# Squares and product stores moved to ScalarE's side, and two pieces of work one step sooner

## The chip, the core and the metric

The kernel runs on one core of one Trainium2 chip. Its time is the device time of that core in microseconds (us), the median of three runs. The engines are TensorE (PE; its weight loads are shown apart as PEld), VectorE (V, or DVE), ScalarE (A, or ACT), GpSimd (G, or POOL) and SyncE (SP). Before the change SP issues every DMA of the program.

## What is computed

The reference has three parts, all in float32:

```python
def sm_attn(qq, kk, vv):
    s = scale * np.matmul(qq, kk.transpose(0, 1, 3, 2))
    s = s - np.max(s, axis=-1, keepdims=True)
    a = np.exp(s)
    a = a / (np.sum(a, axis=-1, keepdims=True) + 1e-09)
    return np.matmul(a, vv)
p_packed = sm_attn(p, k, v)
out = sm_attn(q, p_packed, p_packed)
...
h = np.maximum(x @ w_in, 0.0)
x = h * h @ w_out
...
h = x @ w_in
...
solu = h * sm
...
return (ln @ w_out).astype(np.float32)
```

The attention has 8 batches, 8 heads, 576 positions of 64 numbers, and 32 packed positions. Its output, 4608 tokens of 512 numbers, goes through a first MLP (hidden width 2048, Relu squared) and a second one (hidden width 1024, softmax times h, a layer norm with gains). The weights come as float64 and are decoded to float32 on the chip.

## The kernel before, in words

A float32 matmul is made of three faster ones: each operand is split in a high part (fp32r, a rounded copy) and a low part (the rest), and the products high x high, low x high and high x low are summed. So each operand costs a rounded copy (mostly ACT) and a subtraction (DVE or POOL, `split_lo`, line 55).

**The first MLP's input weights are multiplied by the packed positions' values.** The attention's second half is a matrix `a` (softmax of the queries against 32 packed positions per head) times a small matrix. The kernel multiplies this small matrix by w_in beforehand. A `Unit` (lines 262 to 306) does this for a half `g` of the heads, a slice `s` of 512 columns of w_in and a group `bg` of four batches: it loads a piece of w_in (`raw`), decodes it in three steps (`Decode`, lines 105 to 133: one ACT instruction L122, three DVE instructions L123, L127, L129, then `fin` with a copy on ACT L271 and a subtraction on POOL), and when its `done` time and the packed values allow, `product()` runs 12 matmuls (`pw`), two evacuations on ACT (L293) and two subtractions on DVE (L294). Its result `pws` is stored one step later, from the list `later`: four DMAs of 256 KB to DRAM (`pw_d`), or for slices 0 and 1 of batch 0 four of 64 KB straight into the `slot` tile and three to DRAM (`store`, lines 297 to 306). `load_slot` reads a slice of a batch back from DRAM. There are 16 units for each group of batches; those of group 0 begin at the steps listed in line 514, those of group 1 every second step from step 92 on (line 629).

**The steps.** The main loop (lines 811 to 867) counts t; a step of the first MLP is i = t - 10. At each t the order in which the program is written is: the stores of `later`; the packed attention of batches 0 to 3 (`K0`: `scores`, `soft`, `transp`, `packed`, `pairs`, for t up to 9); `products()`; then `h1` of step i (six matmuls `h`, Relu on ACT L413, r x r on POOL L414, Square into the high part on ACT L415, subtraction on DVE L55); the jobs listed for that t (loads, decodes, softmax jobs); `products()` again; and `ymm` of step i - 4 (12 matmuls `Y`, lines 419 to 443; `LAG` is 4). There are 256 steps: batches 0 and 1 alternate at first, two or four hidden blocks at a time, so step 8 is the first of batch 1.

**The softmax jobs** of a batch `b` and a half `g` (`s2_jobs`, lines 329 to 395) are single instructions or a few: load, scores (`s`), max, subtraction, exponential, sum, normalisation, back-transposition, and the copies to `ah` and `al`, which `h1` reads. For batch 0 they run on DVE, for the others the subtraction, normalisation and low part run on POOL. The jobs of batch 0, half 1 are cut in two parts; the first nine of them are written at t = 9, the others at i = 0. Those of batch 1 are written three at each step from i = 2 to 7 (lines 863 to 865).

**Order.** Instructions wrapped in `pin` (`tc.keep_in_program_order`, line 43) stay behind the instruction that is written just before them for the same engine; these are nearly all matmuls, all DMAs (`dma`, line 51), and ACT's L122 and L293. A planner orders the others by its own model of time. The unit's ready time is in two lines:

```python
self.done = clock[0] + (1 if clock[0] < T0 else 2)   # fin, line 273
return self.done and clock[0] >= self.done and (self.bg, 2 * self.g + 1) in L
```

and `unit_at` (lines 469 to 479) puts a unit's decode steps k, k and k + 1 steps behind its beginning. The units of slice 1 begin at i = -5 (the entries -5 of line 514, written at t = 5).

Of the kernel before, what the change touches and what calls it, by code (L numbers as in the profile page):

```python
# [15 lines left out]
AF = mybir.ActivationFunctionType  # L16
ALU = mybir.AluOpType
# [14 lines left out]
def f(ap):  # L32
    return ap.bitcast(F32)


def build(tc, qT, kT, vP, pT, w_in, w_out, w_in2, w_out2, g_ln, out):
    nc = tc.nc

    TURN = {n: cycle(x) for n, x in {"ETC": "VVA", "LNA": "AAAV"}.items()}
    V, A, G, PE, SP = nc.vector, nc.scalar, nc.gpsimd, nc.tensor, nc.sync  # L40


    pin = tc.keep_in_program_order

    def mm(*a, **k):
        pin(PE.matmul(*a, **k))  # L46

    def flip(own, *a):
        (pin if own else lambda x: x)(PE.transpose(*a))

    def dma(out, in_):
        pin(SP.dma_start(out=out, in_=in_))

    def split_lo(eng, lo, x, hi):
        eng.tensor_tensor(out=lo, in0=x, in1=f(hi), op=ALU.subtract)  # L55

    def pool(name, side="left", space=None):
        st = ExitStack()
        kw = dict(space=space) if space is not None else dict(side=side)
        return st.enter_context(tc.tile_pool(name=name, bufs=1, **kw)), st  # L60
# [3 lines left out]
    pw_d = dr.tile([B, 8, P, 2, 512], F32, name="pw_d")  # L64
# [6 lines left out]
    def bank(name):  # L71
        return ps.tile([P, 512], F32, tag="a", name=name, bufs=4)
# [26 lines left out]
    def t25(k, name, dt=F32):  # L99
        return mp.tile([P, KC * P], dt, tag="e" + k, name=name, bufs=2 if k == "1" else 4)  # L100
# [4 lines left out]
    class Decode:  # L105
        def __init__(self, pl, src, shape, fin, bufs=(3, 2, 3)):
            self.pl, self.shape, self.fin, self.n, self.bufs = pl, shape, fin, 0, bufs
            self.raw = pl.tile([P, shape[0], shape[1], 2], U32, tag="raw", name="raw", bufs=bufs[0])
            dst = self.raw.rearrange("p a c w -> p a (c w)")
            dma(dst if shape[0] > 1 else dst[:, 0, :], src)  # L110
# [33 lines left out]
    class Pack:  # L144
# [71 lines left out]
        def transp(self, n):  # L216
            t = self.pl.tile([P, KC * P], F32, tag="eT", name="eT", bufs=2) if self.own else t25("2", "eT")
            self.eT[n] = t.rearrange("p (k c) -> p k c", k=KC)
            for a, b in ((0, 3), (3, KC)):
                pt = bank("pt")[:, :(b - a) * P]  # L220
                for c in range(a, b):
                    flip(self.own, pt[:, (c - a) * P:(c - a + 1) * P], self.e1[n % 2][:, c * P:(c + 1) * P], ident)
                if next(TURN["ETC"]) == "A":
                    A.copy(t[:, a * P:b * P], pt)
# [37 lines left out]
    class Unit:  # L262
# [34 lines left out]
        def store(self, sf):  # L297
            bg, s, g = self.bg, self.s, self.g
            for b4 in range(4):
                r = slice(32 * b4, 32 * b4 + 32)  # L300
                if bg == b4 == 0 and s < 2:
                    o = f(slot[0, s].rearrange("p g c l x -> p g (c l x)"))
                    for h in range(4):
                        dma(o[32 * h:32 * h + 32, g], sf[r, h])
                else:
                    dma(pw_d[4 * bg + b4, s, :, g].rearrange("(h p) c -> p h c", h=4), sf[r])

    def new_slot(b, s):
        slot[b, s] = big4(ring[0], [P, 2, 2, 2, P], "slot", F32R)
# [90 lines left out]
    def h1(n):  # L400
        b, half, fc = n
        c = slice(half * HF, (half + 1) * HF)
        pb = bank("h1")
        w = slot[b, fc // 2][:, :, fc % 2]
        i = 0
        for g in range(2):
            ah, al = at[b, g]
            for l, x in ((0, ah), (1, ah), (0, al)):
                mm(pb[:, :HF], w[:, g, l], x[:, c], start=(i == 0), stop=(i == 5))
                i += 1  # L410
        rg, g2 = t25("1", "rg"), t25("2", "ghl", F32R)
        r, gg, gh, gl = rg[:, :HF], rg[:, HF:S], g2[:, :HF], g2[:, HF:S]
        A.activation(r, pb[:, :HF], AF.Relu)  # L413
        G.tensor_tensor(out=gg, in0=r, in1=r, op=ALU.mult)  # L414
        A.activation(gh, r, AF.Square)  # L415
        split_lo(V, gl, gg, gh)
        gt[n] = (gh, gl)

    def ymm(n):
        b, half, fc = n  # L420
        gh, gl = gt.pop(n)
        wh, wl = wo[fc]
        firsts = cuts.get(b, whole)
        for oc in range(4):
            o = slice(oc * P, (oc + 1) * P)
            for i, (w, x) in enumerate(((wh, gh), (wl, gh), (wh, gl))):
                mm(Y[oc], w[:, o], x, start=(fc in firsts and i == 0), stop=(fc + 1 in firsts and i == 2))
        if fc + 1 in firsts:
            c0 = b * S + half * HF
            new = (b, half) not in yp  # L430
            if new:
                yp[b, half] = ypp.tile([P, 4 * HF], F32, name=f"yp{half}") if b == 1 else sums()
            t = yp[b, half]
            for oc in range(4):
                o = t[:, oc * HF:(oc + 1) * HF]
                if not new:
                    V.tensor_tensor(out=o, in0=Y[oc], in1=o, op=ALU.add)  # L437
                elif oc % 2 == 0:
                    A.copy(o, Y[oc])
                else:  # L440
                    V.tensor_copy(o, Y[oc])
            if fc == 15:
                later.append(lambda: dma(y_d[:, :, c0:c0 + HF], t.rearrange("p (o c) -> p o c", o=4)))
# [14 lines left out]
    def at_step(i, fn):  # L458
        jobs.setdefault(i if i == "first" else T0 + i, []).append(fn)
# [9 lines left out]
    def unit_at(i, bg, s, g, pl, bufs):  # L469
        d = {}  # L470

        def begin():
            d["u"] = Unit(bg, s, g, pl(), bufs)
            queue.append(d["u"])

        at_step("first" if i == -5 else i, begin)
        k = 3 if i < -5 else 4
        for j in (k, k, k + 1):
            at_step(i + j, lambda: d["u"].d.step())

# [9 lines left out]
    for b in range(2, B):  # L490
# [9 lines left out]
        for s in range(8):  # L500
            i = 16 + 2 * s + 3
            if b == 2:
                i = (17, 19, 21, 23, 25, 31, 33, 35)[s]
            if b == 4:
                i = max(i, 9 + 4 * s)
# [93 lines left out]
    def open_b():  # L599
        era_st.close()  # L600
        atB["p"], atB["st"] = pool("atB")
# [18 lines left out]
    for n in range(8):  # L620
        i = P1 + 1 + PS * n
# [109 lines left out]
    def h2(m):  # L731
# [15 lines left out]
        for i, h in enumerate(t):  # L747
# [16 lines left out]
            G.tensor_tensor(out=rstd, in0=rstd, in1=mhalf, op=ALU.pow)  # L764
            if next(TURN["LNA"]) == "V":
                V.tensor_scalar(out=h, in0=h, scalar1=mv[:, 0:1], scalar2=rstd, op0=ALU.subtract, op1=ALU.mult)
# [27 lines left out]
    def products():  # L794
        while queue and queue[0].ready():
            queue.pop(0).product()

    ps1 = {}
    early = {}
    q0 = {}  # L800

    def load_q(g):
        if g == 0:
            t = sums()
            q0[g] = [t[:, :S], t[:, S:]]
        else:
            q0[g] = [atp.tile([P, S], F32, tag=f"a{c}{g}", name="qf0", bufs=2) for c in "hl"]
        for k in range(2):
            dma(q0[g][k], qT[0, g][:, k])

    for t in range(max(max(j for j in jobs if j != "first"), T0 + N + LAG - 1) + 2):
        i = t - T0
        clock[0] = t
        for fn in later:
            fn()
        later.clear()
        for n in ((0,), (1,), (2,), (3,), (4, 5), (6, 7))[t] if t < 6 else ():
            K0.load_v(n)
        if t + 3 < H:
            K0.load_k(t + 3)  # L820
        if t + 1 < H:
            K0.scores(t + 1)
        if t == 3:
            load_q(0)
        if t == 5:
            load_q(1)
            for j in jobs.pop("first"):
                j()
        if t == H:
            ps0_st.close()  # L830
            ps1["p"], ps1["st"] = pool("ps1", space=PSUM)
            Y += [ps1["p"].tile([P, HF], F32, name=f"Y{o}") for o in range(4)]
        if 0 <= t - 1 < H:
            K0.transp(t - 1)
        if t + 1 < H:
            K0.soft(t + 1)
        if 0 <= t - 2 < H:
            K0.packed(t - 2)
        if t in (4, 6, 8, 9):
            K0.pairs(t // 2 - 2 if t < 9 else 3)  # L840
        if t <= 9:
            products()
        if t == 6:
            for j in s2_jobs(0, 0, q0[0]):
                j()
        if t == 9:
            early[0] = s2_jobs(0, 1, q0[1], 2)
            for j in early[0][:9]:
                j()
            open_b()  # L850
            early[1] = s2_jobs(1, 0), s2_jobs(1, 1)
            for x in early[1]:
                x.pop(0)()
            early[1] = early[1][0] + early[1][1]
        if 0 <= i < N:
            h1(steps[i])
        for j in jobs.get(t, ()):
            j()
        products()
        if i == 0:  # L860
            for j in early[0][9:]:
                j()
        if 2 <= i < 8:
            for j in early[1][3 * i - 6:3 * i - 3]:
                j()
        if 0 <= i - LAG < N:
            ymm(steps[i - LAG])
# [121 lines left out]
```

## Time and profile before

| what | us |
|---|---|
| median of three runs | 1254.64 (1251.4 to 1254.97) |
| the profiled execution, its own time | 1250.78 |
| its span, first to last instruction | 1249.0 |
| PE busy in it | 1159.8 (93%) |
| DVE busy | 874.9 (70%) |
| ACT busy | 639.3 (51%) |
| POOL busy | 610.7 (49%) |

The times of the profile count from the span's start. Busy time leaves out instructions that wait, branch or issue DMAs. "Idle before" is time in which the engine did nothing just ahead of an instruction, with the engine, tile and line that ended it. The granted clock is given as a share of TensorE's full speed, 2.4 GHz; 0.50 is 1.2 GHz. L46 is the line of the matmul helper, L52 that of the DMA helper and L55 that of the subtraction helper, so such rows are told apart by their tiles.

### The profile page before, as it was taken

What the parts mean: (1) busy time and instruction counts of PE and PEld (TensorE: products, weight loads), DVE (VectorE), ACT (ScalarE), POOL (GpSimd) and SP (SyncE); (2) the same over time, 40 slices, a digit from 0 to 9 for tenths busy, and PEclk for the clock granted to TensorE, in tenths of its full rate; (3) what the DMA queues carried; (4) which work ended last, traced back from release to release, by engine and by line L of the source; (5) the groups of instructions that cost most, each with busy time, mean ns of one, the idle gap of its engine ahead of it and who ended that gap; (6) DMA issues with size and microseconds to landing.
All of it is one profiled execution on the core that took longest, in us unless ns stands there. A gap on an engine that the chain in (4) does not pass through costs nothing.

```text
span 1249.0 us, 23478 instructions
## 1 busy us (share of the span) xinstructions
PE 1159.8 (93%) x8556; PEld 1064.5 (85%) x8556; DVE 874.9 (70%) x1722; ACT 639.3 (51%) x1413; POOL 610.7 (49%) x652
## 2 busy tenths in 40 slices
PE   6777699999999989999999999999999899998998
PEld 3456698898999878999999999998888788887888
DVE  4777588755436776575657733449898889989886
ACT  3444455444445554454555544346665556665554
POOL 1055355533324454443434433126886877886853
PEclk9768799999999998999999999999999999999999
DMA  9755777775144889556373482351112111111101
GB/s 329 228 169 141 230 218 231 259 253 189 59 171 148 250 249 305 161 177 250 139 281 134 157 334 104 124 168 35 34 40 64 34 39 63 35 39 42 56 27 43
DMA packets 97540, 187.66 MB, mean 150 GB/s; under 512 B 13968, under 2 KB 41616, under 8 KB 97424
## 3 DMA queue, kind: packets, MB, share of 16 engines
q1 hardware_dynamic: 97424, 186.16, 45.3%
q8 instruction: 67, 1.10, 0.4%
q14 instruction: 49, 0.40, 0.1%
HBM read 119.02 MB, written 66.06 MB: 148 GB/s over the span
## 4 chain that ended last, share of the span: by engine, by line
PE 60%; DVE 13%; POOL 10%; issue 6%; DMA 6%; ACT 4%; SPq 1%; ACTq 0%; DVEq 0%; POOLq 0%
PE Y L46 29%; PE h L46 13%; PE o L712 6%; PE h L712 5%; POOL y L682 3%; POOL cl L892 3%; PE s L46 3%; DMA yf<-y_d 2%; PE pw L46 2%; POOL rstd L764 1%; DVE dw L127 1%; POOL yf L675 1%; DMA raw<-w_out 1%; DVE dw L129 1%; DMA raw<-w_in 1%
## 5 line engine op out<-in xcount | busy, mean ns | idle before, releaser
L46 PE MATMUL Y<-ghl,woh 128*128 128x288 f32 x2048 | 469.4, 305 | 6.2 <-DVE yp L437 4.6
L46 PEld LDWEIGHTS Y<-ghl,woh 128*128 128x128 f32 x2048 | 349.9, 192 | 22.1 <-issue 8.5
L414 POOL TENSOR_TENSOR rg<-rg 128x288 f32<-128x288 f32 x256 | 188.3, 736 | 355.6 <-ACT rg L413 349.2
L46 PE MATMUL Y<-ghl,wol 128*128 128x288 f32 x1024 | 306.7, 300 | 0.0
L55 DVE TENSOR_TENSOR ghl<-rg,ghl 128x288 fp32r<-128x288 f32 x256 | 144.3, 567 | 201.8 <-ACT ghl L415 190.7
L46 PE MATMUL h<-ah,slot 128*128 128x288 f32 x1024 | 219.4, 303 | 24.3 <-ACT ah L388 9.2
L415 ACT ACTIVATE ghl<-rg 128x288 fp32r<-128x288 f32 x256 | 113.8, 445 | 189.3 <-PE Y L46 187.3
L712 PE MATMUL o<-wx,ch 128*128 128x256 f32 x1008 | 192.8, 288 | 8.7 <-ACT ch L891 4.7
L46 PEld LDWEIGHTS Y<-ghl,wol 128*128 128x128 f32 x1024 | 197.0, 192 | 0.0
L46 PEld LDWEIGHTS h<-ah,slot 128*128 128x128 f32 x1024 | 170.8, 195 | 27.6 <-issue 16.1
L712 PEld LDWEIGHTS o<-wx,ch 128*128 128x128 f32 x1008 | 162.5, 194 | 19.8 <-DVE ys L729 7.1
L46 PE MATMUL h<-al,slot 128*128 128x288 f32 x512 | 154.2, 301 | 0.9 <-POOL al L55 0.9
L712 PE MATMUL o<-wx,cl 128*128 128x256 f32 x504 | 143.3, 288 | 3.8 <-POOL cl L892 3.8
L892 POOL TENSOR_TENSOR cl<-raw,ch 128x512 fp32r<-128x512 f32 x84 | 120.3, 1439 | 41.1 <-ACT ch L891 40.9
L413 ACT ACTIVATE rg<-h 128x288 f32<-128x288 f32 x256 | 104.2, 407 | 55.3 <-PE h L46 46.9
L682 POOL TENSOR_TENSOR y<-yf,y 128x256 fp32r<-128x256 f32 x111 | 97.2, 887 | 31.1 <-ACT y L679 29.0
L712 PEld LDWEIGHTS o<-wx,cl 128*128 128x128 f32 x504 | 96.9, 194 | 6.6 <-POOL cl L892 5.3
L46 PEld LDWEIGHTS h<-al,slot 128*128 128x128 f32 x512 | 99.4, 194 | 1.2 <-POOL al L55 1.2
L891 ACT CAST ch<-raw 128x512 fp32r<-128x512 f32 x126 | 76.0, 620 | 39.2 <-DVE raw L897 25.2
L712 PE MATMUL h<-wi,y 128*128 128x512 f32 x312 | 84.2, 404 | 2.0 <-DVE hs L729 1.9
L679 ACT CAST y<-yf 128x256 fp32r<-128x256 f32 x120 | 47.0, 406 | 58.2 <-DVE yf L675 28.5
L55 POOL TENSOR_TENSOR ws<-dw,ws 128x512 fp32r<-128x512 f32 x32 | 41.9, 1312 | 70.4 <-ACT ws L271 70.4
(148 smaller groups left out, 1873.5 us busy)
## 6 DMA issues: line engine op xcount, KB each, us to landing
pw_d<-pws SPq DMA_DIRECT2D x124, 256.0 KB, 4.5
slot<-pw_d SPq DMA_DIRECT2D x62, 512.0 KB, 6.0
raw<-w_in SPq DMA_DIRECT2D x40, 512.0 KB, 6.2
raw<-w_out SPq DMA_DIRECT2D x24, 512.0 KB, 6.4
kf<-kT SPq DMA_DIRECT2D x32, 288.0 KB, 5.1
yf<-y_d SPq DMA_DIRECT2D x36, 256.0 KB, 3.0
out<-ys SPq DMA_DIRECT2D x72, 128.0 KB, 1.7
vf<-vP SPq DMA_DIRECT2D x16, 512.0 KB, 7.0
```

Source lines behind the costliest of these rows:

```text
L46: pin(PE.matmul(*a, **k))
L55: eng.tensor_tensor(out=lo, in0=x, in1=f(hi), op=ALU.subtract)
L127: V.scalar_tensor_tensor(out=x, in0=self.hi, scalar=0x80000000, in1=x, op0=ALU.bitwise_and, op1=ALU.bitwise_or)
L129: V.scalar_tensor_tensor(out=x, in0=self.lo, scalar=29, in1=x, op0=ALU.logical_shift_right, op1=ALU.bitwise_or)
L413: A.activation(r, pb[:, :HF], AF.Relu)
L414: G.tensor_tensor(out=gg, in0=r, in1=r, op=ALU.mult)
L415: A.activation(gh, r, AF.Square)
L679: i = A.copy(c[n][0], x)
L682: (V if YS[cnt[1] % len(YS)] == 'V' else G).tensor_tensor(out=c[n][1], in0=x, in1=f(c[n][0]), op=ALU.subtract)
L712: PE.matmul(bk, x, w[:, y], start=(i == 0), stop=(i == 3 * nk - 1))
L891: A.copy(c[n][0], x)
L892: eng.tensor_tensor(out=c[n][1], in0=x, in1=f(c[n][0]), op=ALU.subtract)
```

## The change

```diff
-    TURN = {n: cycle(x) for n, x in {"ETC": "VVA", "LNA": "AAAV"}.items()}
+    TURN = {n: cycle(x) for n, x in {"ETC": "VA", "LNA": "AAAV"}.items()}
...
-    def dma(out, in_):
-        pin(SP.dma_start(out=out, in_=in_))
+    def dma(out, in_, eng=SP):
+        pin(eng.dma_start(out=out, in_=in_))
...
                     for h in range(4):
-                        dma(o[32 * h:32 * h + 32, g], sf[r, h])
+                        dma(o[32 * h:32 * h + 32, g], sf[r, h], A)
                 else:
-                    dma(pw_d[4 * bg + b4, s, :, g].rearrange("(h p) c -> p h c", h=4), sf[r])
+                    dma(pw_d[4 * bg + b4, s, :, g].rearrange("(h p) c -> p h c", h=4), sf[r], A)
...
         A.activation(r, pb[:, :HF], AF.Relu)
-        G.tensor_tensor(out=gg, in0=r, in1=r, op=ALU.mult)
+        A.activation(gg, r, AF.Square)
         A.activation(gh, r, AF.Square)
...
         at_step("first" if i == -5 else i, begin)
-        k = 3 if i < -5 else 4
+        k = 3 if i < 0 else 4
...
-        if t <= 9:
+        if t < 9:
             products()
...
             early[0] = s2_jobs(0, 1, q0[1], 2)
-            for j in early[0][:9]:
+            for j in early[0][:2]:
+                j()
+            products()
+            for j in early[0][2:9]:
                 j()
...
-        if 2 <= i < 8:
-            for j in early[1][3 * i - 6:3 * i - 3]:
+        if 1 <= i < 6:
+            for j in early[1][4 * i - 4:4 * i]:
                 j()
```

- The float32 square of the first MLP (`gg`) is computed by ACT from the Relu's result instead of by POOL.
- The products' stores are issued from ACT's queue instead of SP's. Being pinned, they stand behind the ACT instruction that is written just before them.
- The two units of slice 1 are decoded at t = 8, 8 and 9 instead of 9, 9 and 10.
- At t = 9 the scores of batch 0, half 1 are written ahead of `products()`, not behind it.
- The softmax jobs of batch 1 are written four at each step from i = 1 to 5.
- The copies of the transposed exponentials (`eT`) go to DVE and ACT in turn, instead of two to DVE and one to ACT.

## Rows read from the trace of the kernel before

**Rows 1.** Busy time by stretch: us of each engine (instructions), granted clock, DMA share, GB/s.

```profile
61.00:155.00 94.00, 67.79 (x402) 60.20 (x401) 66.41 (x106) 42.66 (x95) 43.64 (x42) 0.76 0.62 179
155.00:230.00 75.00, 72.83 (x559) 69.81 (x558) 61.50 (x106) 41.40 (x92) 36.78 (x38) 0.98 0.76 238
397.00:510.00 113.00, 104.30 (x801) 96.64 (x801) 83.29 (x128) 60.66 (x137) 52.91 (x58) 0.97 0.88 259
510.00:815.00 305.00, 303.96 (x2227) 297.22 (x2226) 173.39 (x325) 148.40 (x356) 118.14 (x150) 1.00 0.52 185
```

**Rows 2.** PE's timeline: start, duration, instruction, and idle time before it with its end.

```profile
59.58 0.85 PE L46 MATMUL h<-ah,slot 128*128 128x288 f32 x2 [4.04 <-ACT ah L388]
...
63.77 0.80 PE L46 MATMUL pw<-ws,L 64*128 64x256 f32 x4 [0.21 <-ACT ws L271]
...
70.33 2.19 PE L46 MATMUL s<-qf,slc 128*64 128x288 f32 x8 [0.63 <-DVE pws L294]
...
76.08 0.82 PE L46 MATMUL h<-ah,slot 128*128 128x288 f32 x2 [1.82 <-DMA slot<-pws]
...
81.47 0.82 PE L46 MATMUL h<-ah,slot 128*128 128x288 f32 x2 [4.33 <-DMA slot<-pws]
...
99.89 0.85 PE L46 MATMUL h<-ah,slot 128*128 128x288 f32 x2 [5.13 <-ACT ah L388]
...
147.55 0.82 PE L46 MATMUL h<-ah,slot 128*128 128x288 f32 x2 [6.14 <-DMA slot<-pw_d]
...
468.88 0.58 PE L46 MATMUL pw<-ws,L 64*128 64x256 f32 x1 [2.86 <-ACT rg L413]
```

**Rows 3.** Busy time of two short stretches, columns as in rows 1.

```profile
99.80:106.60 6.80, 5.85 (x23) 5.23 (x23) 5.91 (x5) 2.73 (x7) 5.45 (x6) 0.50 0.41 145
...
468.40:475.30 6.90, 5.66 (x26) 5.14 (x27) 5.14 (x7) 2.92 (x8) 3.63 (x4) 0.51 0.94 286
```

**Rows 4.** SP's own waits up to 815 us: total us, times, longest us.

```profile
SPq L52 <- DVE pws L294: 81.9, 22, 11.7
```

**Rows 5.** SP's timeline: start and duration of the issues.

```profile
39.26 2.52 SPq L52 DMA_DIRECT2D slot<-pws  x4
...
448.70 2.85 SPq L52 DMA_DIRECT2D pw_d<-pws  x4
...
454.12 3.48 SPq L52 DMA_DIRECT2D pw_d<-pws  x4
...
458.75 1.45 SPq L52 DMA_DIRECT2D raw<-w_in  x1
...
483.53 4.23 SPq L52 DMA_DIRECT2D pw_d<-pws  x4
```

**Rows 6.** ACT's timeline at three places, columns as in rows 2.

```profile
42.87 0.31 ACT L239 ACTIVATE pp<-po,r 128x64 fp32r<-128x64 f32 x1 [4.81 <-PE po L235]
...
99.40 0.76 ACT L388 CAST ah<-aT 128x288 fp32r<-128x288 f32 x2 [0.41 <-DVE aT L381]
...
466.04 0.66 ACT L122 ACTIVATE dw<-raw 128x512 f32<-128x512 f32 x1 [5.33 <-DMA raw<-w_in]
```

**Rows 7.** The page's costliest groups: count, busy us, mean ns, idle before.

```profile
L414 POOL TENSOR_TENSOR rg<-rg 128x288 f32<-128x288 f32 x256 | 188.3, 736 | 355.6 <-ACT rg L413 349.2
...
L415 ACT ACTIVATE ghl<-rg 128x288 fp32r<-128x288 f32 x256 | 113.8, 445 | 189.3 <-PE Y L46 187.3
```

**Rows 8.** The stores in the view of tile pws: ns, least, median and most.

```profile
L52 SPq DMA_DIRECT2D pw_d<-pws x124: 302/581/1858, 41.8 to 504.1; - x124
```

**Rows 9.** POOL's timeline ahead of the first step of batch 1.

```profile
93.41 0.95 POOL L414 TENSOR_TENSOR rg<-rg 128x288 f32<-128x288 f32 x1 [1.75 <-ACT rg L413]
...
95.83 1.60 POOL L378 TENSOR_TENSOR t<-t,sm 128x576 f32<-128x576 f32 x1
```

**Rows 10.** Line 414 alone by stretch: POOL's busy us (instructions).

```profile
155.00:230.00 75.00, 19.77 (x25) 0.98 0.76 238
397.00:510.00 113.00, 24.41 (x34) 0.97 0.88 259
```

## The prediction

> **What bounds the kernel now.** I read the table by stretches first [rows 1]. Its stretches split the span by the work of the program: start, first MLP with weights being decoded, and so on. From 510 to 815 us TensorE (PE) is busy 303.96 of 305 us: nothing but less PE work shortens that. After 815 us comes the second MLP, which no edit touches. So the change can gain or lose in two places: from 61 to 230 us, where all but two of the first sixteen products are made beside the first steps, and from 397 to 510 us, where sixteen more are. PE is idle there for 26 us (61 to 155), 2 (to 230) and 9 (397 to 510). ScalarE (ACT) is busy 42.66 of 94 us in the first of these, 41.40 of 75 and 60.66 of 113 in the others.
>
> Next, PE's own timeline with what ended each idle time [rows 2]. The first step waits 4.04 us for ah of group 1. The step that needs the second slice waits 1.82 and 4.33 us for that slice's store to land; ahead of it five waits, 0.21 us the first and 0.63 the last, together 2.7, lie around the second slice's products. The first step of batch 1 waits 5.13 us for ah. A later step waits 6.14 us for a slice read back from DRAM, and in the late stretch a product waits 2.86 us. Around them the granted clock is the lower of its two levels, 1.2 GHz: 0.50 from 99.8 to 106.6, 0.51 from 468.4 to 475.3 us [rows 3].
>
> Last, the queues. SP's own waits: 81.9 us, in 22 waits, on the DVE subtraction that ends a product [rows 4]. Loads stand behind these stores. In the late stretch a load of w_in is issued only at 458.75 us [rows 5]; the four stores that went ahead of it on SP began at 454.12 and took 3.48. ACT idled 5.33 us for its landing [rows 6], and PE's 2.86 follow.
>
> **The squares.** 256 multiplications of 736 ns leave GpSimd (POOL), 256 Squares come to ACT [rows 7]. A Square of this size takes 445 ns; two ACT copies of this size in a row take 0.76 us together [rows 6], so one more in a row costs some 0.36 (between 0.76 - 0.445 and 0.445). In a step ACT does Relu, then the new Square, then the old one, which comes 0.36 later. PE uses it four steps on, and ACT's old Square already sits idle 189.3 us in total before it, 187.3 of it for PE's Y. That idle time covers the new 256 x 0.36 = 92 us: cost 0 where ACT isn't full (510 to 815: ACT 148.40 of 305 [rows 1], and 122 steps make 44 more). Without the cover, it would be 0.36 per step. A gain on DVE, from having no POOL multiplication beside it, I bound at 0 to 3 us and take as 0 by itself, since PE's waits already count it.
>
> **The stores.** 124 stores to DRAM and 16 into slices (four for each of four units) change their queue. On SP one to DRAM takes 302 ns at least and 581 in the median [rows 8]; groups of four take 2.85 us after a pause of the queue, 3.48 right behind a load, once 4.23, and four slice stores 2.52 [rows 5]. ACT showed no issue, so its price is bounded: from 4 x 0.302 = 1.2 us a group to 3.48 (4.23 for one, not for all). I take 2.4: the quiet group of 2.85, nearest to a queue of their own, less an instruction of 0.445 that may still run when the first is issued. What stands behind a group is the next Relu and both Squares, then decode and evacuation; these wait also for DVE's subtraction, and PE waits for them through its PSUM banks. On SP the loads of raw weights no longer stand behind stores. Loads of slices still wait for the stores to land.
>
> **The sum, term by term.**
> A, start and first step. The first unit's seven stores now lie in ACT's idle 4.81 us ahead of an evacuation at 42.87 [rows 6]. On SP they start at 39.26; 2.52 for four, and 2.1 for three by the quiet group, make 43.9: a spill of 1. Two decodes one step sooner add DVE and ACT work to this busy end of the start. The scores ahead of the product bring ah forward by that product's time on PE, but put the product, its stores and their landing back by the scores' 2.19 (as those at 70.33 [rows 2]). The first step needs both; a gain can be at most 2 of its 4.04 us wait. +2 (-2 to +5).
> B, second slice. Decode and ready time come one step sooner and, by the rule in the code (a done unit waits one step before step 0, two after), the products two. The five small waits (2.7) and the two for the landing (6.15) make 8.9 at most; ACT's issue, behind the last part's ah, keeps some: -5 (-8.9 to 0).
> C, second batch. Group 1's scores start two steps sooner and all ends at i = 5, not 7. On POOL its normalisation of 1.60 us stood behind, among others, a multiplication of 0.95 [rows 9], which goes. The wait is 5.13, and PE's 5.85 busy us at the low clock would be 2.9 less: 8.0 at most. -7 (-8.0 to 0); what is late next is the decode chain, with the 6.14 us wait at 147.55, which I leave as it is (-6 to +5).
> D, 155 to 230. ACT 41.40 + 25 x 0.36 + 8 x 2.4 = 69.6 of 75 us (25 and 34 multiplications lie in the two stretches [rows 10]; the eight and sixteen units are the list's), beside PE's 72.83. Tight, so bursts show: +2 (0 to +8).
> E, 397 to 510. ACT 60.66 + 34 x 0.36 + 16 x 2.4 = 111.3 of 113. Relief for the load that comes late: 2.86 and half of PE's 5.66 at low clock, 5.7 at most; I take 4, since the DMA engines are 0.88 busy in this stretch and landing stays slow. ACT's fullness gives 4 back. 0 (-6 to +15).
> The copies of eT: every second, not every third, on ACT, five or six more of 32, each near the 0.445 of [rows 7]. 0 (-1 to +1).
> Sum: +2 - 5 - 7 + 2 + 0 = -8. The profiled execution took 1250.78 us (span 1249.0), which is 3.9 below the median of three, 1254.64. -8 makes 1242.8 of it, and 1246.6 of the median, which I predict.
>
> **Rivals.**
> First, ACT becomes the bound (slower). Place: the late stretch. By the middle of the seen groups, 3.2 us (between 2.85 and 3.48), ACT needs 60.66 + 12.2 + 51.2 = 124 in a stretch of 113: +11; four more in D, with B and C half as good (-6) and A at +2: +11 in all, 1265.6. It decides from a group price of about 2.4 us: 17 pairs of steps in 113 us are 6.65 each, of which ACT uses 3.57 and 0.72 for new Squares, and a unit comes every second step. For it: groups of 2.85 and above in every row. Against it: ACT may run up to four steps behind PE, and idles much today. Chance 0.30.
> Second, a wash: the early waits only move to the decode chain and to the slice that is read back, or the planner, which orders all but the pinned instructions by its own model, leaves the sooner jobs where they were. Then B and C return 4, E loses its relief and A and D cost what they do: +2 - 4 + 2 + 0 to 4, between 0 and +4: about 1256.6 at +2. Chance 0.20.
> Beside it stands a rule of the Trainium skill, "DMA: Bandwidth & Descriptors", section "Issuing engines are not separate DMA queues": a second issuing engine saves only the sequencer's time to begin a transfer, usually small. By that rule E's relief would be 0 and the sum -4. The trace of before disagrees in part: SP's waits of 81.9 us are no issue time, and loads stood behind them.
>
> **How the numbers follow.** About 0.3%, 3.8 us, is what a measurement can tell from no change. Faster than 1250.9: the forecast, 0.50. Within: the wash, 0.20. Above 1258.4: the first rival, 0.30. The range goes down to 1232 (E's relief whole, the wait at 147.55 gone, B and C near their bounds), and up to 1268, just above the first rival. The forecast's own range is 1232 to 1251.
>
> **What would show it.** In the changed profile: POOL without the multiplication, 256 more Squares on ACT; the store groups in ACT's queue at 2.4 us or less for B to E, 3 or more for the first rival. The waits of 4.33 and 5.13 us gone, the first batch-1 step near 90 us, not 99.9; the 4.04 there or longer by up to 2. From 397 to 510 the stretch as long as now, with no decode waiting 5 us for w_in. PE waiting there for ACT's Relu or evacuation, and a longer stretch, would make the forecast wrong; so would a first batch-1 step that starts at 99 us as now.

## The result and the profile after

The changed kernel takes 1263.41 us (median of four runs, 1261.88 to 1265.65), the kernel before 1254.31 beside it: a ratio of 1.0079, 95% interval 1.0056 to 1.0101. I had forecast 1246.6. The sign is wrong; the first rival's 1265.6 is near what came, though only in part for its reason. The profiled execution took 1262.98 us, its span is 1261.2, 12.2 longer than before.

Where the time goes is seen best by steps. Below is the time in us at which the Relu of each step starts (ACT's rows of line 413 counted from 0), before and after, and in four kernels of the experiments: stores back on SP (e1), squares alone (e5), a POOL multiplication added to e1 (e7), and the stores on POOL (e9).

| step | before | after | e1 | e5 | e7 | e9 |
|---|---|---|---|---|---|---|
| 0 | 60.9 | 64.4 | 62.6 | 60.1 | 62.8 | 66.0 |
| 8 | 102.7 | 92.3 | 93.1 | 99.6 | 94.6 | 94.5 |
| 16 | 137.9 | 138.5 | 126.3 | 133.8 | 133.7 | 134.0 |
| 24 | 167.9 | 162.1 | 157.1 | 163.7 | 165.3 | 158.1 |
| 40 | 216.2 | 220.4 | 203.6 | 209.7 | 213.7 | 203.7 |
| 48 | 240.5 | 242.3 | 228.4 | 232.8 | 238.3 | 225.0 |
| 96 | 384.6 | 385.5 | 373.2 | 376.0 | 383.0 | 368.2 |
| 128 | 494.3 | 509.2 | 480.8 | 481.9 | 493.2 | 479.3 |
| 248 | 794.1 | 805.9 | 778.8 | 780.2 | 791.3 | 776.0 |
| end | 1249.0 | 1261.2 | 1235.6 | 1235.8 | 1245.8 | 1232.8 |

After is 10.4 us ahead of before at step 8, 5.8 ahead at step 24, and 1.8 behind at step 48. Steps 96 to 128, with most of the sixteen products of group 1, take 14.0 more. From 128 to 248, where PE sets the pace, it gains 3.1.

Steps 24 to 40 and 96 to 128 in the table by stretches, first before, then after (busy us and instructions of PE, PEld, DVE, ACT and POOL, granted clock, DMA share, GB/s):

```profile
167.90:216.20 48.30, 46.13 (x350) 44.16 (x349) 40.76 (x70) 26.91 (x62) 25.30 (x26) 0.96 0.78 242
...
384.60:494.30 109.70, 100.78 (x778) 93.21 (x777) 81.91 (x126) 59.59 (x135) 51.76 (x56) 0.97 0.81 241
```

```profile
162.10:220.40 58.30, 51.03 (x363) 46.88 (x364) 41.60 (x76) 34.80 (x81) 12.98 (x10) 0.97 0.74 220
...
385.50:509.20 123.70, 106.56 (x786) 97.53 (x785) 74.71 (x128) 71.29 (x169) 29.55 (x24) 0.94 0.75 218
```

POOL's and DVE's work falls (from 51.76 to 29.55 and from 81.91 to 74.71), and still the late stretch is 14.0 us longer. PE idles 17.1 us of it, not 8.9, and its busy time rises by 5.8, at a mean granted clock of 0.94 instead of 0.97. Two stretches of it now run at the lower of the two levels, where the kernel before had one [rows 3]; after's two, same columns:

```profile
409.10:415.90 6.80, 5.13 (x26) 4.94 (x27) 3.60 (x6) 2.30 (x5) 1.29 (x2) 0.50 0.71 217
494.40:501.20 6.80, 6.11 (x29) 5.60 (x30) 4.17 (x6) 2.37 (x7) 1.24 (x1) 0.50 0.36 81
```

ACT's busy time doesn't count DMA issues. They stand in its timeline as ACTq (start, duration, instruction, idle time before it and its end; the row of 177.53 is the fourth store of the row of 173.92, seen by itself):

```profile
173.92 3.92 ACTq L52 DMA_DIRECT2D pw_d<-pws  x4
...
177.53 0.31 ACTq L52 DMA_DIRECT2D pw_d<-pws  x1
177.88 0.41 ACT L413 ACTIVATE rg<-h 128x288 f32<-128x288 f32 x1 [3.98 <-DMA pw_d<-pws]
...
461.35 0.32 ACTq L52 DMA_DIRECT2D pw_d<-pws  x1
461.62 0.44 ACT L413 ACTIVATE rg<-h 128x288 f32<-128x288 f32 x1
461.70 4.71 ACTq L52 DMA_DIRECT2D pw_d<-pws  x3
466.46 0.45 ACT L414 ACTIVATE rg<-rg 128x288 f32<-128x288 f32 x1 [4.40 <-issue]
...
485.40 4.61 ACTq L52 DMA_DIRECT2D pw_d<-pws  x4
490.06 0.44 ACT L414 ACTIVATE rg<-rg 128x288 f32<-128x288 f32 x1 [4.54 <-DMA raw<-w_in]
...
504.47 0.31 ACTq L52 DMA_DIRECT2D pw_d<-pws  x1
504.66 0.44 ACT L415 ACTIVATE ghl<-rg 128x288 fp32r<-128x288 f32 x1
504.81 0.45 ACTq L52 DMA_DIRECT2D pw_d<-pws  x1
...
505.29 0.70 ACTq L52 DMA_DIRECT2D pw_d<-pws  x1
...
506.03 1.30 ACTq L52 DMA_DIRECT2D pw_d<-pws  x1
507.38 0.44 ACT L415 ACTIVATE ghl<-rg 128x288 fp32r<-128x288 f32 x1 [1.39 <-PE Y L46]
```

A Relu or a Square that is ready stands still while the stores ahead of it in the queue are issued. A group can also pause inside itself: of the 3.92 us at 173.92 only 1.95 are issues, and the fourth store begins 1.9 us after the third has ended, when an earlier store has landed, by the releaser that the profile names. At 485.40 the issues are 1.4 of 4.61 us. From 385.5 to 509.2 us ACT's queue pauses in this way for 7.5 us ahead of stores, 2.2 for DVE's subtraction and 5.3 for transfers to land.

The four stores of a group in a free queue take 0.31, 0.45, 0.70 and 1.30 us, 2.76 in all; 5.0 at 461.35. Single durations of the 56 stores from 398 to 507 us add up to 41.1 us, 2.94 for each of the 14 groups; 5.8 of them run beside an instruction of ACT (71.3 busy and 41.1 of issue cover 106.6 us), so a group takes 2.5 us of ACT's own, without the pauses. (The expectations below count 15 groups of 2.74, the same 41.) The view of tile pws has them all (ns: least, median, most; first and last start), as [rows 8] has them on SP:

```profile
L52 ACTq DMA_DIRECT2D pw_d<-pws x124: 309/544/2022, 40.6 to 517.7; - x124
...
L52 ACTq DMA_DIRECT2D slot<-pws x16: 514/601/871, 38.0 to 75.7; - x16
```

PE's timeline, columns as in [rows 2]:

```profile
62.53 0.82 PE L46 MATMUL h<-ah,slot 128*128 128x288 f32 x2 [6.85 <-DMA slot<-pws]
...
77.87 0.72 PE L46 MATMUL h<-ah,slot 128*128 128x288 f32 x2 [1.40 <-DMA slot<-pws]
...
90.56 0.53 PE L46 MATMUL h<-ah,slot 128*128 128x288 f32 x2 [1.30 <-ACT ah L388]
...
178.35 0.53 PE L46 MATMUL h<-ah,slot 128*128 128x288 f32 x2 [1.65 <-ACT rg L413]
...
410.77 1.62 PE L46 MATMUL pw<-ws,L 64*128 64x256 f32 x11 [2.81 <-DVE pws L294]
```

The waits of 4.33 and 5.13 us [rows 2] shrank to 1.40 and 1.30; the first step's 4.04 grew to 6.85, for its slice's store. At 178.35 PE waits 1.65 us for the very Relu that the group at 173.92 held up. The two largest of PE's waits from 385.5 to 509.2 (total us, times, longest), and below them the only one that e1, with the stores on SP, has in its steps 96 to 128:

```profile
PE pw L46 <- DVE pws L294: 6.7, 6, 2.8
PE pw L46 <- ACT ws L271: 4.4, 3, 1.6
```

```profile
PE pw L46 <- DVE pws L294: 6.0, 4, 3.3
```

So the wait for DVE's subtraction is there without the moved stores too. What they add is waits for ACT: 4.4 us for a copy of decoded weights and four smaller ones, 7.9 in all, where e1 has none.

Last, the chain and the costliest groups of after (count, busy us, mean ns, idle before):

```profile
PE 52%; DVE 14%; POOL 9%; ACT 8%; issue 7%; DMA 5%; ACTq 4%; SPq 0%; DVEq 0%; POOLq 0%
...
L415 ACT ACTIVATE ghl<-rg 128x288 fp32r<-128x288 f32 x256 | 113.3, 442 | 117.4 <-PE Y L46 104.3
...
L414 ACT ACTIVATE rg<-rg 128x288 f32<-128x288 f32 x256 | 114.0, 445 | 34.5 <-issue 18.2
```

ACT's queue is 4% of the chain, and 18.2 us of the idle time before the new Square end with "issue": the instruction waited for nothing but the queue. The old Square's idle time fell from 189.3 [rows 7] to 117.4: the new one fills what was free.

### The profile page after: what moved, and what is told of

Read it like the earlier page. It is cut to its first block, busy times and chain, and to the rows that moved or that the text cites. A ratio compares the mean times of both kernels' runs of the same rounds, so it can differ in the third digit from the quotient of the medians.

```text
span 1261.2 us, 22939 instructions
## 1 busy us (share of the span) xinstructions
PE 1160.6 (92%) x8556; PEld 1061.3 (84%) x8556; DVE 835.4 (66%) x1716; ACT 739.4 (59%) x1675; POOL 423.6 (34%) x396
## 3 DMA queue, kind: packets, MB, share of 16 engines
q10 hardware_dynamic: 18624, 33.56, 10.4%
## 4 chain that ended last, share of the span: by engine, by line
PE 52%; DVE 14%; POOL 9%; ACT 8%; issue 7%; DMA 5%; ACTq 4%; SPq 0%; DVEq 0%; POOLq 0%
PE Y L46 26%; PE h L46 12%; PE o L712 5%; PE h L712 4%; ACTq L52 4%; POOL cl L895 3%; POOL y L682 3%; PE s L46 2%; DMA pw_d<-pws 2%; DMA yf<-y_d 2%; DVE dw L127 2%; DVE dw L129 1%; POOL rstd L764 1%; ACT dw L122 1%; POOL yf L675 1%
## 5 line engine op out<-in xcount | busy, mean ns | idle before, releaser
L55 DVE TENSOR_TENSOR ghl<-rg,ghl 128x288 fp32r<-128x288 f32 x256 | 135.5, 530 | 231.3 <-ACT ghl L415 230.9
L46 PE MATMUL h<-ah,slot 128*128 128x288 f32 x1024 | 215.8, 299 | 14.3 <-DMA slot<-pws 8.2
L415 ACT ACTIVATE ghl<-rg 128x288 fp32r<-128x288 f32 x256 | 113.3, 442 | 117.4 <-PE Y L46 104.3
L46 PEld LDWEIGHTS h<-ah,slot 128*128 128x128 f32 x1024 | 167.8, 192 | 16.9 <-issue 8.6
L414 ACT ACTIVATE rg<-rg 128x288 f32<-128x288 f32 x256 | 114.0, 445 | 34.5 <-issue 18.2
L367 POOL TENSOR_TENSOR t<-t,mx 128x576 f32<-128x576 f32 x14 | 16.5, 1182 | 217.3 <-DVE mx L364 217.3
```

Of the source, the lines that this page charges most:

```text
L367: E.tensor_tensor(out=t(), in0=t(), in1=over(mx()), op=ALU.subtract)
L414: A.activation(gg, r, AF.Square)
```

## The experiments

All times are medians beside the kernel before on the same chip; its own medians there were 1253.3 to 1255.1, so differences between runs of different chips carry up to some 2 us of that.

**Which part costs, which gains.** e1: the changed kernel with the stores back on SP.

```diff
-                        dma(o[32 * h:32 * h + 32, g], sf[r, h], A)
+                        dma(o[32 * h:32 * h + 32, g], sf[r, h], SP)
...
-                    dma(pw_d[...], sf[r], A)
+                    dma(pw_d[...], sf[r], SP)
```

> The changed kernel with its products' stores issued from SP again; everything else of the change stays. Theory T1 (the stores' issue fills ACT in the late stretch): steps 96 to 128 go from 123.7 us back to 108 to 112, ACT without issues there holds about 71 us, and the time is 1245 to 1252. Rival T2 (the new Squares, 0.36 us a step, fill ACT): steps 96 to 128 stay at 118 or more, the time at 1256 or more. Rival T3 (the pieces written sooner disturb the order): steps 8 to 48 still lose the 10 us that steps 0 to 8 gained, and the time stays above 1254.

Measured: 1236.96 us, ratio 0.9866 (0.9845 to 0.9887). That is theory T1's side, and 8 us below its range. Without the moved stores the change is a gain of 18 us; the stores on ACT cost 26.4. Steps 24 to 40 and 96 to 128 of it, columns as above:

```profile
157.10:203.60 46.50, 44.82 (x350) 42.67 (x350) 37.97 (x70) 33.51 (x78) 12.18 (x10) 1.00 0.83 251
373.20:480.80 107.60, 101.51 (x775) 94.53 (x774) 75.14 (x126) 72.44 (x166) 29.22 (x24) 0.95 0.84 245
```

ACT has the same work as after, 72.44 us, in a stretch that is 16.1 us shorter.

e2: the changed kernel with the multiplication back on POOL.

```diff
-        A.activation(gg, r, AF.Square)
+        G.tensor_tensor(out=gg, in0=r, in1=r, op=ALU.mult)
```

> The changed kernel with the float32 square on GpSimd again; the stores stay in ACT's queue. T1: ACT loses some 32 x 0.36 = 12 us of its 106.6 us (instructions and issues) in steps 96 to 128, but the groups of stores still hold the Relu and Squares behind them, so the stretch is 115 to 122 us and the time 1255 to 1261. T2: the stretch falls to 112 or less and the time to 1252 or less.

Measured: 1279.89 us, 1.0213 (1.0193 to 1.0232), 16.5 above the changed kernel and above both ranges, which had no room for a loss when the squares go back. Steps 96 to 128 take 126.8 us with ACT busy for only 59.64 of them, 96.7 with the issues:

```profile
396.80:523.60 126.80, 108.39 (x787) 98.73 (x786) 81.74 (x128) 59.64 (x136) 52.89 (x56) 0.93 0.74 214
```

So the late stretch isn't long because ACT's time is used up: with a lighter ACT it is longer still. (The moved stores' own price is the same with either place of the squares: 26.4 us here, and 1279.89 - 1252.11 = 27.8 against e4 below.)

e3: the changed kernel with group 1's stores on SP and group 0's on ACT.

```diff
-                    dma(pw_d[...], sf[r], A)
+                    dma(pw_d[...], sf[r], A if bg == 0 else SP)
```

> The changed kernel with only the stores of group 1 (steps 96 to 131) issued from SP; those of group 0 stay in ACT's queue. T1: up to step 96 as in the changed kernel (385.5 us), steps 96 to 128 in 108 to 112 us, so the time is 1248 to 1252. T2: steps 96 to 128 take 118 us or more, time 1257 or more. Compared with the kernel that has all stores on SP it also gives what the early stores cost or gain on ACT's queue: by T1 a loss of 0 to 6 us.

Measured: 1248.02 us, 0.9956 (0.9933 to 0.9979). Of the 26.4 us, 15.4 are group 1's stores (1263.41 - 1248.02) and 11.1 group 0's (1248.02 - 1236.96), more than the 0 to 6 expected of these.

e4: the kernel before with the pieces that come one step sooner (decode, scores ahead of the product, four jobs at a step), neither squares nor stores nor copies of eT moved. e5: the kernel before with the squares on ACT alone.

> The kernel before with only the sooner pieces: slice 1's decode one step sooner, the scores ahead of the product at t = 9, batch 1's softmax jobs four at a step from i = 1. Stores on SP, float32 square on GpSimd, eT as before. T1: step 8 starts at 93 to 97 us (102.7 before), half of that is lost again by step 48, the late stretch is as before (109.7), time 1246 to 1252. T3 (the sooner pieces bring nothing or do harm): 1254 or more, with step 48 at 240 us or later.

> The kernel before with the float32 square on ACT and nothing else. Additive theory A (the parts act on their own: stores +26, sooner pieces -3, squares and eT the rest): time 1238 to 1243, steps 8 to 48 some 8 us and steps 96 to 128 some 5 us shorter than before (137.8 and 109.7). Rival I (the squares pay only together with the sooner pieces): 1248 or more.

Measured: e4 1252.11 us, 0.9981 (0.9962 to 1.0): a gain of 3 us by the medians, between none and 4.8. e5 1238.64 us, 0.9882 (0.9853 to 0.9912): a gain of 14.6, as additive theory A had it, though its steps 8 to 48 and 96 to 128 are 4.6 and 3.8 us shorter, not 8 and 5. From e4 to e1, which differ by the squares and the copies of eT, it is 15.2. So the parts act on their own: the squares bring as much without the sooner pieces as with them, and the stores cost as much with either place of the squares. The sum, -3 (sooner), -15 (squares), +26.4 (stores), is +8.4, against +9.1 measured; along before, e4, e1 and after it holds by construction. The copies of eT were not tried alone.

**Why the squares gain.** e7: e1 with a multiplication on POOL in the first 136 steps whose result nothing reads. e8: e1 with a Square on ACT there that nothing reads.

```diff
         A.activation(gg, r, AF.Square)
+        if clock[0] < T0 + 136:
+            pin(G.tensor_tensor(out=dm, in0=r, in1=r, op=ALU.mult))
```

```diff
         A.activation(gg, r, AF.Square)
+        if clock[0] < T0 + 136:
+            pin(A.activation(dm, r, AF.Square))
```

> The kernel with all of the change but the stores (on SP), and an extra multiplication of the Relu's result on GpSimd in steps 0 to 135, of the same size as the one that was removed, written to a tile that nobody reads. ACT still makes the squares. Theory P (what the squares' move brought is a GpSimd that stands in nobody's way: its own queue and DVE beside it): most of the 15 us come back, time 1246 to 1252, DVE busier by 3 to 7 us in steps 96 to 128. Rival W (what it brought is a shorter chain Relu, square, subtraction): no change, 1235 to 1240.

> The kernel with all of the change but the stores (on SP), and a second extra Square on ACT in steps 0 to 135, written to a tile that nobody reads: 136 x 0.36 = 49 us more on ACT. Theory C (ACT's idle time covers one Square more a step while the stores are elsewhere): 1237 to 1240. Rival F (ACT is near full even so): every Square lies on the path in the stretches with products, some 72 steps, up to +26 us: 1245 to 1263.

Measured: e7 1248.92 us, 0.996 (0.9938 to 0.9981); e8 1237.84 us, 0.9873 (0.9845 to 0.9901). The unread multiplication gives back 12.0 of the 15 us; the unread Square costs 0.9. So most of the gain is POOL's release, not a shorter way from Relu to Square, and ACT's free time covers even one more Square a step, as long as no issue stands in it. Steps 96 to 128, first e7, then e8:

```profile
383.00:493.20 110.20, 102.54 (x778) 95.41 (x777) 80.89 (x126) 72.16 (x167) 53.72 (x56) 0.95 0.82 239
```

```profile
376.00:484.30 108.30, 101.40 (x777) 93.91 (x776) 75.27 (x126) 82.44 (x198) 29.56 (x24) 0.97 0.84 243
```

With POOL's multiplication back, DVE's 126 instructions take 80.89 us, not 75.27 (75.14 in e1): they are the same instructions, and longer. Of the 5.7 us against e1 5.4 are in the decode's instructions. Its line 127 from 60 to 520 us in the view of groups, and line 294, the subtraction that reads a product from PSUM, first e1, then e7 (whose lines stand two lower):

```profile
L127 DVE SCALAR_TENSOR_TENSOR dw<-raw,dw 128x512 uint32<-128x512 uint32 x46 | 34.6, 753 | 1.0
...
L294 DVE TENSOR_TENSOR pws<-pw,pws 128x512 fp32r<-128x512 f32 x60 | 39.2, 683 | 13.0 <-ACT pws L293 12.1 <-DMA pw_d<-pws 0.6
```

```profile
L129 DVE SCALAR_TENSOR_TENSOR dw<-raw,dw 128x512 uint32<-128x512 uint32 x45 | 41.4, 922 | 1.0
...
L296 DVE TENSOR_TENSOR pws<-pw,pws 128x512 fp32r<-128x512 f32 x60 | 39.2, 684 | 13.7 <-ACT pws L295 12.7 <-DMA pw_d<-pws 0.6
```

Not every row is longer: the decode's line 129, of the same kind as 127, stays at 792 and 791 ns, its line 123 goes from 547 to 629, and line 294 stays as it is.

The Trainium skill, "Perfetto Trace Analysis", section "Optimizing Scalar/DVE Operations", says that GpSimd and DVE share a port of the SBUF, so that moving work between these two may not help. The lengthened rows agree with that, and so does e12: the square on DVE is hardly better than on POOL (0.9966 against e4's 0.9981, with intervals that overlap).

e12: the change with the stores on SP and the square on DVE.

```diff
-        A.activation(gg, r, AF.Square)
+        V.tensor_tensor(out=gg, in0=r, in1=r, op=ALU.mult)
```

> The whole change with the stores on SP and the float32 square on VectorE in place of ScalarE. Theory P (the gain of the squares is GpSimd's release): it stays where VectorE has room; VectorE is busy 75.2 of 107.6 us in steps 96 to 128 and gets 32 x about 0.45 = 14 more, 90 in all, but 64.8 of 94 us at the start, where it is already the busiest beside TensorE: 1238 to 1246 us, taken as 1242. Rival Q (VectorE is what limits the early steps, and the gain was that VectorE ran faster without GpSimd beside it): the square's own time on VectorE gives all of it back: 1249 to 1256 us.

Measured: 1249.31 us, 0.9966 (0.9952 to 0.998), in rival Q's range. With POOL free and the square on DVE, 4.4 of e1's gain of 18 us are left. How much of e7's 12 us is DVE's longer instructions, and how much POOL's own decodes and normalisations standing behind the multiplication, these runs don't separate. e12 shows that more time on DVE can lose as much, but with 11.6 us more of it in steps 96 to 128 (86.75 against 75.14), where e7 has 5.7, and in other places: against e1, e7 is 9.9 us behind by step 48 and loses 2.6 more from 96 to 128, e12 5.2 and 3.6. And POOL's queue has a part of its own: in steps 8 to 16 of e7 PE waits for POOL's subtraction of decoded w_out (tile wol), in e1 not at all:

```profile
PE Y L46 <- POOL wol L55: 3.0, 2, 1.6
```

**What an issue costs, and where.** e10: the changed kernel with each store to DRAM cut in two.

```diff
-                    dma(pw_d[...], sf[r], A)
+                    for h2 in range(2):
+                        dma(pw_d[... half h2 ...], sf[r, 2 * h2:2 * h2 + 2], A)
```

> The changed kernel with each of the 124 stores to DRAM made of two halves, both issued from ACT: twice the issues, the same bytes. Theory R (a group holds ACT until its bytes can be taken, 2.7 us for 1 MB): the issues of a group take 2.7 to 3.2 us together and the time is 1260 to 1267. Rival N (an issue has a price of its own, 0.3 to 0.55 us): the groups take 4 us or more, steps 96 to 128 grow by 16 us or more, and the time is 1285 or more.

Measured: 1302.77 us, 1.0392 (1.0356 to 1.0427), as rival N had it. The same bytes in twice the DMAs cost 39 us more. The stores in the view of tile pws, and steps 96 to 128:

```profile
L52 ACTq DMA_DIRECT2D pw_d<-pws x248: 309/443/1821, 41.8 to 554.5; - x124
```

```profile
404.60:541.60 137.00, 112.99 (x790) 103.28 (x788) 72.25 (x127) 69.59 (x166) 29.61 (x24) 0.89 0.69 199
```

The issues of that stretch add up to 57.0 us instead of 41.1: not double, since half a store is cheaper than a whole one; and the stretch is longer by 13.3 us for 15.9 more of issue (rival N had 16 or more), so its length goes with the issue time.

e9: the changed kernel with the stores issued from POOL's queue (`G` in place of `A`).

> The whole change, with the 140 stores issued from GpSimd's queue in place of ScalarE's. Theory N (an issue holds up only what stands behind it in its own queue, and costs where that queue is full): GpSimd is busy 29.2 of 107.6 us in steps 96 to 128 of the version with stores on SP, and 15 groups of 2.74 us make 41 more, 70 of 107, so most of it is covered; its subtractions and normalisations are late by up to one group: 1237 to 1246 us, taken as 1241. Rival R (what costs is that loads no longer stand behind stores, so that both collide in the DMA engines, whichever second queue issues the stores): as long as the changed kernel, 1258 to 1266 us.

Measured: 1232.63 us, 0.9833 (0.9801 to 0.9866). That is theory N's side, and lower than its range; rival R has fallen, for here too no load stands behind a store. The stores in the view of tile pws, some of POOL's timeline, and steps 24 to 40 and 96 to 128 (the issues count as POOL's busy time here):

```profile
L52 POOL DMA_DIRECT2D pw_d<-pws x124: 550/550/772, 40.9 to 487.6; - x124
...
418.36 1.29 POOL L55 TENSOR_TENSOR ws<-dw,ws 128x512 fp32r<-128x512 f32 x1 [2.90 <-issue]
420.33 2.18 POOL L52 DMA_DIRECT2D pw_d<-pws  x4 [0.68 <-DVE pws L294]
422.52 1.17 POOL L378 TENSOR_TENSOR t<-t,sm 128x576 f32<-128x576 f32 x1
...
158.10:203.70 45.60, 44.67 (x351) 42.75 (x350) 38.97 (x70) 33.59 (x78) 23.43 (x30) 1.00 0.91 281
368.20:479.30 111.10, 103.85 (x782) 96.26 (x782) 77.11 (x128) 73.38 (x168) 59.91 (x80) 0.95 0.79 241
```

An issue takes 0.55 us on POOL, hardly ever more, 2.2 for a group. With the issues POOL has work for 59.91 of 111.1 us, and behind a group stands a decode's subtraction or a normalisation, not the step's Relu. Between e9 and e1 the intervals overlap, so which of these two queues is better isn't shown by this pair. Nor does e9 show which difference from ACT counts: the 56 issues of steps 96 to 128 take 31.4 us on POOL, not 41.1, none of its pauses there ends with a transfer that lands, and what stands behind a group is another instruction. Stores written at another place of ACT's queue, behind a step's Squares, would part these; that was not run.

**A better version.** e13: group 0's stores on POOL, group 1's on SP. e14: the kernel before with squares on ACT and stores on POOL, without the sooner pieces.

> The whole change, with the stores of group 0 issued from GpSimd's queue and those of group 1 from SP's. If the steps add up as in the two versions it is made of (step 96 begins at 368.2 us with all stores on GpSimd's queue, steps 96 to 128 take 107.6 us with all on SP's, against 111.1), the time is 3 us under that of all stores on GpSimd's queue: 1227 to 1231 us, taken as 1229. Rival: the late stretch ends with SP's loads whichever way the start went, and the difference of 3.5 us there is scatter: 1231 to 1238 us.

> The kernel before with the squares on ScalarE and the stores on GpSimd's queue, without the pieces that come one step sooner. If those pieces are worth 2 to 3 us, as the two pairs of runs with stores on SP have it: 1235 to 1239 us. Rival: with SP free of the stores, the sooner decode at last finds its loads landed, and the pieces are worth 5 to 10 us: 1239 to 1245 us.

Measured: e13 1233.52 us, 0.983 (0.9815 to 0.9846); e14 1243.04 us, 0.9914 (0.9894 to 0.9934). e13's time lies in its rival's range and can't be told from e9, though its steps 96 to 128 are the 106.0 us that were hoped for: of the rival's reason the trace shows nothing. e14's time lies in its rival's range too: with the stores on POOL the sooner pieces, with the copies of eT, are worth some 10 us (step 48 starts at 231.9 us in e14, at 225.0 in e9), against 2 to 3 with them on SP. Why, no run separates. e9 and e13 beat both kernels, e9 the kernel before by 1.7%.

## Why the prediction was wrong, step by step

**E, 397 to 510 us, is the step that failed**: "ACT's fullness gives 4 back. 0 (-6 to +15)". Steps 96 to 128 came out 14.0 us longer, near the end of the term's own range; group 1's stores alone make 15.4 us of the time (e3) and 16.1 of the stretch (123.7 against e1's 107.6), where the term had 4. The count in it was near: I had 2.4 us a group and 111.3 us of ACT work in the stretch (with 16 groups, of which the stretch of before holds 15 products), and a group takes 2.5 us, ACT 106.6 of 123.7 us with busy time and issues. Not counted were the 7.5 us in which the queue pauses ahead of a store. What failed above all is the conclusion that work which fits costs little. A sum says nothing about order: a group stands between a step's Relu and its Squares, or ahead of an evacuation, and what is ready there waits for 2 to 5 us at a time. Two runs bear that out against "ACT is full": with a lighter ACT the stores cost as much (e2), and with a busier ACT and no issues in it nothing is lost (e8). That it is the issues and not the bytes, e10 shows: the same bytes with more issue time lose more.

**E's relief** of 4 us for the late load came to nothing that the time shows. SP no longer waits for products, but for the buffers of the loads and for stores to land (SP's own waits up to 815 us, after):

```profile
SPq L52 <- DVE dw L129: 136.6, 27, 13.4
SPq L52 <- DMA pw_d<-pws: 120.8, 21, 14.7
```

Stores on SP (e1, e13) and on POOL (e9) take 107.6, 106.0 and 111.1 us for steps 96 to 128. In this stretch the rule of the Trainium skill that I weighed ("DMA: Bandwidth & Descriptors", section "Issuing engines are not separate DMA queues") was nearer than I: no relief that the time shows. And in the changed kernel the time that SP's queue saved was spent in ACT's.

Some relief lies earlier, where I had counted none. Between steps 40 and 48 of e1 a decode waits for its load, on ACT's timeline:

```profile
219.28 0.67 ACT L122 ACTIVATE dw<-raw 128x512 f32<-128x512 f32 x1 [3.41 <-DMA raw<-w_out]
```

In the other kernels with all stores on SP (before, e4, e5) that wait is 1.7 to 2.1 us; with the early stores on ACT or POOL (after, e3, e9, e13, e14) none is there, and steps 24 to 48 take 66.9 us in e9, 71.3 in e1.

**D, 155 to 230 us**, had +2 (0 to +8). Steps 24 to 40 alone took 10.0 us more than before; without the stores on ACT they take 46.5. The prediction's ACT sum of 69.6 of 75 us "fits" here too, and fails for the same reason.

**A** was +2 (-2 to +5): step 0 starts 3.5 later, as worked out, with the slice's store late. **B and C** were -5 and -7: step 8 starts at 92.3 us, "near 90" as the text wanted, and A to C stand at -10.4 where I had -10. But they aren't kept. By step 16 nothing is left (5.8 us come back by step 24, where the changed kernel has no wait for the slice that is read back), and e4 shows that even with the stores on SP the sooner pieces end at -3. Its profiled execution, the slowest of ten, starts step 8 5.9 us ahead of before and step 48, at 239.3 us, 1.2 ahead. In part that is the second rival's mechanism: the early wait moves to the slice that is read back, 6.14 us before [rows 2], now 8.14:

```profile
143.50 0.82 PE L46 MATMUL h<-ah,slot 128*128 128x288 f32 x2 [8.14 <-DMA slot<-pw_d]
```

C named that wait (-6 to +5) and left it out of its -7. What takes the rest back isn't shown.

**The squares**: cost 0 was right (e8: 0.9 for one more). The gain on DVE, which "I bound at 0 to 3 us and take as 0 by itself, since PE's waits already count it", was put at nothing; the move of the squares measured 15, and e7's multiplication alone gives 12.0 of it back. This is the second failed term. I looked for the gain in PE's waits of two or three places; it lies in DVE's instructions along the decode, 5.7 us of them in steps 96 to 128 (e7 against e1, where the stretch is 2.6 us longer), and in POOL's queue, in parts that the runs don't separate.

The first rival had the right sign and nearly the number (+11, measured +9.1), but that was luck, from errors that cancel: stores 17 in its terms (11 + 4 + 2), measured 26.4; squares 0, measured -15; sooner pieces -6, measured -3. Its condition, a group price above some 2.4 us, was just met at 2.5 (2.94 by the issues' own durations), but its mechanism, an ACT with more work than time, was not.

## What to carry to other kernels

In these runs a DMA issue takes the time of the queue that it is written in, and what is ready behind it waits. So choose the queue by how soon the instruction behind the issue is needed, and not by the room that a busy sum leaves. When a queue's instructions go straight to the engine that sets the pace, count the longest pause, not the mean load. And when work leaves GpSimd, look for the gain in VectorE's durations, with an unread instruction put back to measure it, before taking it as nothing.

## What was not expected of the hardware

- Four stores of 256 KB in a row from ACT's queue get dearer one by one, 0.31, 0.45, 0.70, 1.30 us in a group without pauses, and up to 2.02; from POOL's queue each is 0.55, 0.77 at most.
- Stores issued from POOL's queue ran beside a DVE busy for 77 of 111 us, and no issue took over 0.77 us. The Trainium skill, "SBUF — State Buffer", section "SBUF: two separate sides", warns that a DMA issued from GpSimd's queue starves while DVE runs an operation in a 2-port performance mode, which locks the port they share. Here no such starving is seen: the stores landed 5.0 us after their issue in the median, against 4.7 from SP (e1) and 4.5 from ACT. Whether any of DVE's operations here ran in such a mode, no run shows.
- One unread POOL multiplication a step, of 0.74 us, costs the kernel 12.0 us in 136 steps; one unread ACT Square, of 0.43 us, costs 0.9, which is within the noise.
- POOL's multiplication lengthened DVE's line 127 from 753 to 922 ns, and left the subtraction that reads PSUM at 683 and 684.
